# The sign factor of converted weight words: two VectorE comparisons, or two ScalarE signs and a GpSimd sum

## The chip, the cores and the metric

The kernel runs on one core of a Trainium2 chip. The core has five engines that run side by side, each through its own queue and strictly in the order written: TensorE (PE, matrix products, with its weight loads shown apart as PEld), VectorE (DVE), ScalarE (ACT), GpSimd (POOL) and SyncE (SP, which here only issues transfers). They wait for each other through semaphores. The metric is the device time of one execution in microseconds; lower is better.

## The reference

Three layers follow each other. Everything is float32, and the weights of the layers reach the kernel as float64 where the reference drew them so.

```python
scores = scale * np.matmul(q, k.transpose(0, 1, 3, 2))      # 4 x 8 heads, 576 x 576
thresh = np.max(scores, axis=-1, keepdims=True) - tau
scores = np.where(scores >= thresh, scores, -1e9)            # softmax over what is left, times v
...
expert_idx = np.argmax(x @ w_gate, axis=1)                   # one of 8 experts for each of 2304 tokens
h = np.maximum(xe @ w1[e], 0.0);  ye = h @ w2[e]             # 512 -> 1024 -> 512
out[mask] = gate_w[mask, None] * ye
...
h = x @ w_in                                                 # last layer, 512 -> 2048 -> 512
g = h - np.tanh(h)
return (g @ w_out).astype(np.float32)
```

`w_in` and `w_out` of the last layer are the subject here. They are float64 (the drawn float32 array is multiplied by a float64 scalar), so each weight comes in as two 32-bit words.

## The kernel before, in words

The program has three stages. Attention fills the time to about 345 us. A routing step (to about 370 us) sorts the tokens by expert. Then a loop over steps `g` runs the experts (`g` below `GE` = 72, from 370 to about 650 us) and the last layer (to the end). In one expert step PE computes `h` (L1040, 12 matmuls) for hidden block `g` and then `y` (L1095, 12 matmuls) for hidden block `g-2`. All products are made from a high and a low part of each factor, so every tile is split: ACT rounds to the high part, DVE or POOL subtracts to get the low part.

- `relu(g)`: ACT writes the high part `hh` from the PSUM tile `h` (L1075), DVE the low part `hl` (L1076: one operand in PSUM, one in SBUF). Only then is the PSUM tile free. `h` has two banks, so `h` of step `g+2` waits for L1076 of step `g`.
- `wload` (SP, L1002) and `wsplit`: weights of an expert are loaded four or five steps ahead and split two or three steps ahead (L1008 on ACT, L1010 on DVE for `w1` and on POOL for `w2`).
- `gather_exp` (POOL, L1057), `trans` (PE, L1017), `evac` (ACT L1027, DVE L1031) bring the next expert's tokens in.
- `conv`: the float64 words of the last layer's weights are turned into float32 in 32 chunks of 128 x 512 weights, and stored in DRAM (`wscr`) for the last layer. All 32 run between 370 and 627 us, in the expert stage, at steps written in the table `TB["conv"]`, with `TB["cv"]` = 0, 3, 4, 5: `load` at the chunk's step, `bits` three steps later, `sign` one after that, `store` one more.

In a chunk, `lo` and `hi` are the two words of each weight (every second element of the tile `cv`), `hf` is `hi` read as a float32, and `m` is half of the tile `cm`. `bits` builds the magnitude's bits in `lo` (L1155 writes a part into `m`, L1157 joins it with `lo`) and then starts the sign factor in `m`: L1159 writes 1 where `hf` is at most -T. `sign` takes the absolute value of the joined word on ACT (L1163), completes the factor on DVE (L1164: 1 where `hf` is at least T, less what L1159 wrote, so the factor is 1, -1 or 0), and multiplies both on POOL (L1166). `store` is an SP transfer (L1169) that waits for POOL; SP's weight loads for the next step stand behind it.

There is no scheduler: instructions stand on each engine's queue in the order in which the Python code emits them. Within a step this is `relu(g)`, then the list for the step (token evacuation, weight loads and splits, then the chunk's functions), then `y` of `g-2`. So on ACT what `sign` emits stands in front of the next step's L1075, and on DVE what `bits` emits stands in front of the next step's L1076.

Of the kernel before, what the change touches and what calls it, by code (L numbers as in the profile page):

```python
# [11 lines left out]
F32 = mybir.dt.float32  # L12
# [5 lines left out]
AF = mybir.ActivationFunctionType  # L18
ALU = mybir.AluOpType
# [447 lines left out]
class Moe:  # L467
# [110 lines left out]

    def hilo(self, T, x):
        V = self.nc.vector  # L580
        ab = T([128, 2, NTL], I32)
        V.tensor_scalar(out=ab[:, 0], in0=x, scalar1=7, scalar2=None, op0=ALU.logical_shift_right)
        V.tensor_scalar(out=ab[:, 1], in0=x, scalar1=127, scalar2=None, op0=ALU.bitwise_and)
        return ab[:, 0], ab[:, 1]

    def route(self, K, T, psum):

# [24 lines left out]
        cnt = self.cnt = inc[:, :, NTL]  # L612
        key, cmp, rank = T([128, E]), T([128, E, E]), T([128, E])
        sel, em = K([128, E, E]), T([128, E, E])
        self.sel = sel
        rm, rv = T([128, 2, E, E]), K([128, 2, E])
        self.eid = cp.tile([128, E], I32, name="eid")
# [295 lines left out]
def quads():  # L913

    r = sorted((x for x in np.roots(COEF[::-1]) if x.imag > 0), key=lambda x: x.real)
    return [float(v) for x in r for v in (-x.real, x.imag ** 2)] + [COEF[4]]


class Mlp(Moe):
    def run(self, ctx):  # L920
        nc, tc = self.nc, self.tc
        sp = self.sp = ctx.enter_context(tc.tile_pool(name="m", bufs=1))
        pp = self.pp = ctx.enter_context(tc.tile_pool(name="mp", bufs=1, space=PSUM))
        self.kn = quads()
        self.ab = self.cp.tile([128, 2], F32, name="kna")
        for i in range(2):
            nc.gpsimd.memset(self.ab[:, i:i + 1], self.kn[2 * i])
        self.sched, self.cm = {}, None
        self.hs, self.ys, self.W, self.xs, self.xr, self.evs, self.regs = {}, {}, {}, {}, {}, {}, {}
        self.keep = sp.tile([128, 3072], F32, tag="lxa", name="keep")  # L930
        self.free = sp.tile([128, max(6 * NMAX, 8 * NW)], F32, tag="lxb", name="free")
        K = Carve(self.keep)
        self.route(K, Carve(self.free), self.psum)
        self.hbuf = sp.tile([128, max(6 * NMAX, 8 * NW)], F32R, tag="lxb", name="hbuf")
        for fn in self.early():
            fn()
        for m in range(-(-PASS[0][2] // 128)):
            self.gather_exp(0, m, min(128, PASS[0][2] - 128 * m))
        self.early2()
        n = iter(range(12))  # L940
        self.overflow(lambda: sp.tile([128, 1024], F32R, **(dict(tag="xa", bufs=8) if next(n) < 8 else dict(tag="we", bufs=4)), name="wo"), self.psum)
        self.plan(K)
        g0 = int(min(self.sched)) - 1
        ny = g0 - LY
        for g in range(g0, GE + GL + 1):
            if g >= 0:
                if g < GE:
                    self.relu(g, g // 8, self.h_exp(g // 8, g % 8))
                elif g < GE + GL:
                    self.act(g, self.h_last(*divmod(g - GE, 16)))  # L950
                if GE < g <= GE + GL:
                    self.act2(g - 1)
            for fn, a in self.sched.get(g, []):
                fn(*a)
            if g - GE - GL + 16 in SKIP:
                ny -= 1
            elif LY <= g < GE + GL:
                self.y_mm(ny)
            ny += 1
            for fn, a in self.sched.get(g + 0.5, []):  # L960
                fn(*a)
        for g in range(ny - 1, GE + GL - MLAST):
            self.y_last(g)
        for m in range(MB):
            for g in range(GE + GL - MLAST, GE + GL):
                self.y_last(g, [m])
# [170 lines left out]

    def conv(self, i, h):
        nc = self.nc
        T = 3.4332275390625e-05  # L1140
        st = {}

        def load():
            t = self.sp.tile([128, 1024], F32R, tag="cv", name="cv", bufs=3).bitcast(U32)
            nc.sync.dma_start(out=t.rearrange("p (a b) -> p a b", a=2) if i < 8 else t, in_=self.src64[i][h])
            r = t.rearrange("p (n t) -> p n t", t=2)
            st["lo"], st["hi"] = r[:, :, 0], r[:, :, 1]
            st["hf"] = st["hi"].bitcast(F32)
            if self.cm is None:
                self.cm = self.sp.tile([128, 1024], F32R, tag="cm", name="cm")  # L1150
            st["m"] = self.cm.bitcast(F32)[:, 512 * h:512 * h + 512]

        def bits():
            m = st["m"].bitcast(U32)
            nc.vector.tensor_scalar(out=m, in0=st["hi"], scalar1=3, scalar2=0x40000000,  # L1155
                                    op0=ALU.logical_shift_left, op1=ALU.bitwise_xor)
            nc.vector.scalar_tensor_tensor(out=st["lo"], in0=st["lo"], scalar=29, in1=m,  # L1157
                                           op0=ALU.logical_shift_right, op1=ALU.bitwise_or)
            nc.vector.tensor_scalar(out=st["m"], in0=st["hf"], scalar1=-T, scalar2=None, op0=ALU.is_le)  # L1159

        def sign():
            c = st["lo"].bitcast(F32)
            nc.scalar.activation(out=c, in_=c, func=AF.Abs)  # L1163
            nc.vector.scalar_tensor_tensor(out=st["m"], in0=st["hf"], scalar=T, in1=st["m"],  # L1164
                                           op0=ALU.is_ge, op1=ALU.subtract)
            nc.gpsimd.tensor_tensor(out=st["m"], in0=st["lo"].bitcast(F32), in1=st["m"], op=ALU.mult)  # L1166

        def store():
            nc.sync.dma_start(out=self.wscr[i, :, 512 * h:512 * h + 512], in_=st["m"])  # L1169

        return [load, bits, sign, store]


# [185 lines left out]
```

## Time and profile before

| | |
|---|---|
| median of 3 runs | 1077.41 us (1076.29 to 1078.05) |
| the profiled execution | 1076.63 us |
| its span, first to last instruction | 1074.5 us |
| mean granted TensorE clock | 0.944 |
| busy over the span | PE 957.3, PEld 876.6, DVE 895.3, ACT 671.5, POOL 730.7 us |

The span is what the profile's times count from; 2.1 us of the execution lie around it. A busy share is an average over the whole program; the chunks' 32 instances of each instruction lie in the 270 us from 370 to 640, so that stretch is to be read apart. Two instructions on one engine may overlap by about 0.1 us at their borders, since the next one starts while the one before drains. A duration in the timeline begins when the engine starts an instruction, so time for which the instruction is held up inside, with no semaphore to wait for, is part of it.

### The profile page before, as it was taken

To read this page: it belongs to the slowest core of one execution; us is meant where nothing else is said; L and a number is where in the kernel's file an instruction comes from. 1 tells how busy PE (TensorE), PEld (TensorE's weight loads), DVE (VectorE), ACT (ScalarE), POOL (GpSimd) and SP (SyncE) were. 2 spreads that over 40 slices of the span, in tenths; PEclk is the share of its full clock that TensorE was granted. 3 is DMA by queue.
4 is the path that set the end of the run, shared out by engine and by line. 5 is a ranking of instruction groups with operands and counts; after the bars stand their busy time and mean duration, and the time that the engine had idled before them with its cause. 6 is when DMAs were issued, how large, how long until landed. Compare 5 with 4: busy or idle time off the path is not lost.

```text
span 1074.5 us, 20770 instructions
## 1 busy us (share of the span) xinstructions
PE 957.3 (89%) x7342; PEld 876.6 (82%) x7342; DVE 895.3 (83%) x1635; ACT 671.5 (62%) x1262; POOL 730.7 (68%) x645
## 2 busy tenths in 40 slices
PE   4688897887787488999999988999999999999997
PEld 3576786776677387989999988888999999998986
DVE  5899888888884698977798876998989889888894
ACT  5797887986974154444455557666665666656662
POOL 3897887886874364455656567787867768677763
PEclk9698888898988599999999999999999999999999
DMA  6798999998989485877787976220101101000000
GB/s 160 145 213 165 211 205 152 225 202 163 175 155 169 149 292 199 278 227 247 258 290 252 295 247 177 76 76 20 40 8 38 30 20 40 8 31 1 20 11 30
DMA packets 247368, 153.16 MB, mean 143 GB/s; under 512 B 179642, under 2 KB 222028, under 8 KB 247261
## 3 DMA queue, kind: packets, MB, share of 16 engines
q1 hardware_dynamic: 243501, 141.02, 53.2%
q0 software_dynamic: 3312, 10.49, 2.8%
q8 instruction: 59, 0.97, 0.4%
q14 instruction: 48, 0.39, 0.1%
q10 hardware_dynamic: 448, 0.30, 0.1%
HBM read 85.08 MB, written 23.60 MB: 101 GB/s over the span
## 4 chain that ended last, share of the span: by engine, by line
PE 50%; DVE 9%; issue 3%; DMA 2%; ACT 1%; POOL 0%; another core or an unknown queue 0%; POOLq 0%; DVEq 0%; SPq 0%; ACTq 0%
PE h L1040 25%; PE y L1123 15%; PE y L1095 9%; DVE w L1236 2%; DVE w L1237 2%; PE t L1017 1%; DVE w L1234 1%; DMA xr<-rows,idx 1%; DVE cv L1157 1%; DVE tm L1235 1%; DVE w L1238 1%; DMA raw<-in_moe_w_dram 1%; DVE w L1010 1%; DMA raw<-wscr 0%; DVE cm L1159 0%
## 5 line engine op out<-in xcount | busy, mean ns | idle before, releaser
L265 POOL TENSOR_TENSOR e<-em,e 128x1024 f16<-128x1024 f32 (+1 forms) x98 | 158.1, 1613 | 55.0 <-ACT e L261 23.5
L1233 POOL TENSOR_SCALAR tm<-u 128x384 uint8<-128x384 f32 x88 | 129.7, 1474 | 51.4 <-ACT u L1229 50.8
L1040 PE MATMUL h<-xa,w 128*128 128x256 f32 (+6 forms) x864 | 140.5, 313 | 7.6 <-DVE hbuf L1076 6.8
L1095 PE MATMUL y<-hbuf,w 128*128 128x256 f32 (+6 forms) x864 | 139.5, 310 | 0.6 <-ACT yo L1098 0.6
L1040 PEld LDWEIGHTS h<-xa,w 128*128 128x128 f32 x864 | 130.5, 194 | 9.9 <-DVE hbuf L1076 8.1
L240 ACT ACTIVATE e<-sps,n 128x576 f32<-128x576 f32 x144 | 110.6, 768 | 34.8 <-DVE n L234 33.7
L1010 POOL TENSOR_TENSOR w<-raw,w 128x1024 fp32r<-128x1024 f32 x36 | 91.8, 2551 | 56.0 <-ACT w L1008 28.8
L1095 PEld LDWEIGHTS y<-hbuf,w 128*128 128x128 f32 x864 | 127.5, 191 | 1.3 <-ACT yo L1098 0.8
L1236 DVE SCALAR_TENSOR_TENSOR w<-y,w 128x384 f32<-128x384 f32 x96 | 123.3, 1284 | 0.0
L1229 ACT ACTIVATE u<-h 128x384 f32<-128x384 f32 x96 | 47.1, 491 | 117.3 <-PE h L1040 116.4
L253 DVE SCALAR_TENSOR_TENSOR em<-sps,n,e 128x576 f32<-128x576 f32 x144 | 116.6, 810 | 4.0 <-ACT e L240 2.4
L234 DVE TENSOR_REDUCE n<-sps 128x1 f32<-128x576 f32 x144 | 107.1, 744 | 12.3 <-PE sps L226 11.8
L1250 POOL TENSOR_TENSOR gl<-w,gh 128x384 fp32r<-128x384 f32 x83 | 85.7, 1032 | 38.0 <-ACT gh L1249 38.0
L1040 PE MATMUL h<-xk,w 128*128 128x384 f32 x576 | 109.6, 338 | 0.7 <-DVE w L1010 0.5
L297 PE MATMUL ops<-vh,et 128*128 128x64 f16 (+1 forms) x2240 | 97.4, 201 | 13.0 <-DVE x L303 12.1
L1040 PEld LDWEIGHTS h<-xk,w 128*128 128x128 f32 x576 | 102.1, 188 | 5.6 <-DVE w L1010 1.3
L297 PEld LDWEIGHTS <-et 128*128 128x128 f16 (+1 forms) x2240 | 83.6, 107 | 25.3 <-issue 21.1
L261 ACT CAST e<-em 128x576 f16<-128x576 f32 x144 | 99.9, 695 | 1.2 <-DVE em L253 1.2
L1075 ACT ACTIVATE hbuf<-h 128x256 fp32r<-128x256 f32 (+6 forms) x72 | 31.2, 433 | 108.3 <-PE h L1040 108.2
L226 PE MATMUL sps<-ka,qa 128*128 128x288 f32 x320 | 87.7, 367 | 9.4 <-DVE em L253 5.7
L1008 ACT CAST w<-raw 128x1024 fp32r<-128x1024 f32 x72 | 75.6, 1051 | 21.4 <-DVE free L597 11.6
L1123 PE MATMUL y<-w,gh 128*128 128x512 f32 x258 | 81.1, 395 | 3.2 <-POOL w L1010 1.5
(228 smaller groups left out, 2296.8 us busy)
## 6 DMA issues: line engine op xcount, KB each, us to landing
raw<-in_moe_w_dram SPq DMA_DIRECT2D x64, 512.0 KB, 5.2
cv<-in_moe_w_in_dram SPq DMA_DIRECT2D x16, 512.0 KB, 5.0
cv<-in_moe_w_out_dram SPq DMA_DIRECT2D x16, 512.0 KB, 5.4
wscr<-cm SPq DMA_DIRECT2D x32, 256.0 KB, 3.2
raw<-wscr SPq DMA_DIRECT2D x16, 512.0 KB, 3.8
xw<-yT SPq DMA_DIRECT2D x24, 192.0 KB, 2.7
vv<-in_v_dram SPq DMA_DIRECT2D x8, 512.0 KB, 5.1
raw<-in_q_dram SPq DMA_DIRECT2D x6, 576.0 KB, 7.7
```

The source lines that it names most:

```text
L234: nc.vector.tensor_reduce(out=n[:, 0:1], in_=ps[:, :, 0:288], axis=AX.XY, op=ALU.max, negate=True)
L240: nc.scalar.activation(out=e, in_=ps[:, :, 0:288], func=AF.Exp, bias=n[:, 0:1])
L253: nc.vector.scalar_tensor_tensor(out=self.em[u, g][:, i].rearrange("p (a b) -> p a b", a=2), in0=ps[:, :, 0:288], scalar=n[:, 1:2], in1=e, ...
L261: self.nc.scalar.copy(self.e16[u, g][:, i, 0:S], self.em[u, g][:, i])
L265: eng.tensor_tensor(out=e16[:, r, S + 64:], in0=em[:, r, 0:512], in1=e16[:, r, 0:512], op=ALU.subtract)
L297: nc.tensor.matmul(o[q], lhsT=et[:, base + c, q], rhs=vh[:, a, j, c if c < 5 else c - 5, :], start=(n == 0), stop=(n == len(terms) - 1))
L1010: (self.nc.gpsimd if pool else self.nc.vector).tensor_tensor(out=l, in0=raw, in1=h.bitcast(F32), op=ALU.subtract)
L1040: self.nc.tensor.matmul(out, lhsT=a, rhs=b, start=(i == 0), stop=(i == len(parts) - 1))
L1095: nc.tensor.matmul(self.ys[d], lhsT=a[:, f % 2, s], rhs=b, start=(f == 0 and i == 0), stop=(f == 7 and i == 2))
L1123: nc.tensor.matmul(self.ys[m], lhsT=a[:, s], rhs=b[:, f % 2], start=(f == 0 and i == 0), stop=(f == 15 and i == 2))
L1233: nc.gpsimd.tensor_scalar(out=mk, in0=u, scalar1=RCUT * RCUT, scalar2=None, op0=ALU.is_gt)
L1236: V.scalar_tensor_tensor(out=w, in0=y, scalar=b, in1=w, op0=ALU.add, op1=ALU.mult)
```

## The change

Both DVE comparisons go. A small tile `knt` (`tt2`) gets two constants per partition, -T' and T', T' being the float32 just below T. In `sign`, ACT takes the sign of `hf` - T' into `m`, then the sign of `hf` + T' in place into `hf`, then the absolute value with the factor 0.5. POOL adds both signs (2, 0 or -2) and then multiplies as before. `bits` keeps L1155 and L1157.

```diff
@@ Mlp.run
+        T = float(np.nextafter(np.float32(3.4332275390625e-05), np.float32(0)))
+        self.tt2 = self.cp.tile([128, 2], F32, name="knt")
+        for i in range(2):
+            nc.gpsimd.memset(self.tt2[:, i:i + 1], T if i else -T)
@@ conv
-        T = 3.4332275390625e-05
@@ conv, bits
-            nc.vector.tensor_scalar(out=st["m"], in0=st["hf"], scalar1=-T, scalar2=None, op0=ALU.is_le)
@@ conv, sign
-            nc.scalar.activation(out=c, in_=c, func=AF.Abs)
-            nc.vector.scalar_tensor_tensor(out=st["m"], in0=st["hf"], scalar=T, in1=st["m"],
-                                           op0=ALU.is_ge, op1=ALU.subtract)
+            nc.scalar.activation(out=st["m"], in_=st["hf"], func=AF.Sign, bias=self.tt2[:, 0:1])
+            nc.scalar.activation(out=st["hf"], in_=st["hf"], func=AF.Sign, bias=self.tt2[:, 1:2])
+            nc.scalar.activation(out=c, in_=c, func=AF.Abs, scale=0.5)
+            nc.gpsimd.tensor_tensor(out=st["m"], in0=st["m"], in1=st["hf"], op=ALU.add)
             nc.gpsimd.tensor_tensor(out=st["m"], in0=st["lo"].bitcast(F32), in1=st["m"], op=ALU.mult)
```

The order of DVE before, at the chunk whose `bits` lie at 457.9 us in the profile (`hbuf<-h` is L1076, `w<-raw,w` the low part of an expert's weights, `keep` and `tok` small tiles of the routing):

```order
L1155 TENSOR_SCALAR cm<-cv 128x512
L1157 SCALAR_TENSOR_TENSOR cv<-cv,cm 128x512
L1159 TENSOR_SCALAR cm<-cv 128x512
L1076 SCALAR_TENSOR_TENSOR hbuf<-h,hbuf 128x416
L1010 TENSOR_TENSOR w_7274<-raw,w_7273 128x1024
L756 TENSOR_SCALAR keep<-h 128x18
L570 TENSOR_TENSOR tok_7383<-h,keep 128x18
L1164 SCALAR_TENSOR_TENSOR cm<-cv,cm 128x512
L1155 TENSOR_SCALAR cm<-cv 128x512
```

The same place on DVE now (line numbers are 3 or 4 higher: L1158 was L1155, L1160 was L1157, L1080 was L1076, L1014 was L1010):

```order
L1158 TENSOR_SCALAR cm<-cv 128x512
L1160 SCALAR_TENSOR_TENSOR cv<-cv,cm 128x512
L1080 SCALAR_TENSOR_TENSOR hbuf<-h,hbuf 128x416
L1014 TENSOR_TENSOR w_7286<-raw,w_7285 128x1024
L756 TENSOR_SCALAR keep<-h 128x18
L570 TENSOR_TENSOR tok_7396<-h,keep 128x18
L1158 TENSOR_SCALAR cm<-cv 128x512
```

The low part of the hidden tile now stands directly behind the second `bits` instruction, and nothing of `sign` is left on DVE.

ACT before, at the same place (L1163 is the absolute value, L1075 the high part of the hidden tile, L1008 an expert's weights):

```order
L1075 ACTIVATE hbuf<-h 128x416
L1008 CAST w_7273<-raw 128x1024
L1163 ACTIVATE cv<-cv 128x512
L1075 ACTIVATE hbuf<-h 128x416
L1027 CAST xa<-t 128x2x128 x2
```

ACT now (L1165 and L1166 are the two signs, L1167 the absolute value, L1079 was L1075):

```order
L1079 ACTIVATE hbuf<-h 128x416
L1012 CAST w_7285<-raw 128x1024
L1165 ACTIVATE cm<-cv,knt 128x512
L1166 ACTIVATE cv<-cv,knt 128x512
L1167 ACTIVATE cv<-cv 128x512
L1079 ACTIVATE hbuf<-h 128x416
L1031 CAST xa<-t 128x2x128 x2
```

Three instructions instead of one stand in front of the next step's hidden tile. On POOL each of the 32 multiplications gets the sum directly in front of it.

## Rows read from the trace of the kernel before

**Rows 1.** The profile page, the chain that ended last, by engine

```profile
PE 50%; DVE 9%; issue 3%; DMA 2%; ACT 1%; POOL 0%; another core or an unknown queue 0%; POOLq 0%; DVEq 0%; SPq 0%; ACTq 0%
```

**Rows 2.** Busy time by stretch: PE, PEld, DVE, ACT, POOL; granted clock; DMA share; GB/s

```profile
370.00:640.00 270.00, 255.53 (x1757) 250.67 (x1758) 223.01 (x320) 131.01 (x244) 152.36 (x89) 0.98 0.79 260
460.00:470.00 10.00, 7.47 (x39) 7.00 (x39) 9.60 (x14) 3.27 (x7) 5.13 (x5) 0.83 0.86 269
```

**Rows 3.** Waits of PE, 375 to 640 us: total, times, longest

```profile
PE h L1040 <- DVE hbuf L1076: 6.8, 4, 2.5
```

**Rows 4.** Groups, 375 to 640 us: count, busy us, mean ns, idle before

```profile
L1166 POOL TENSOR_TENSOR cm<-cv,cm 128x512 f32<-128x512 f32 x32 | 44.2, 1382 | 55.8 <-issue 16.6 <-ACT hbuf L1075 14.8 <-DVE cm L1164 9.9
...
L1159 DVE TENSOR_SCALAR cm<-cv 128x512 f32<-128x512 f32 x32 | 28.8, 900 | 1.1
L1164 DVE SCALAR_TENSOR_TENSOR cm<-cv,cm 128x512 f32<-128x512 f32 x32 | 28.4, 891 | 0.0
...
L1163 ACT ACTIVATE cv<-cv 128x512 f32<-128x512 f32 x32 | 22.0, 687 | 21.8 <-DVE cv L1157 12.4 <-issue 5.2 <-POOL cm L1166 3.4
```

**Rows 5.** Timeline at 459 us: start, duration, engine, instruction, idle before

```profile
459.06 1.83 PE L1095 MATMUL y<-hbuf,w 128*128 128x288 f32 x12
...
460.10 2.77 DVE L1159 TENSOR_SCALAR cm<-cv 128x512 f32<-128x512 f32 x1
...
460.21 2.36 POOL L1010 TENSOR_TENSOR w<-raw,w 128x1024 fp32r<-128x1024 f32 x1
...
462.79 0.58 DVE L1076 SCALAR_TENSOR_TENSOR hbuf<-h,hbuf 128x416 fp32r<-128x416 f32 x1
...
463.42 4.09 PE L1040 MATMUL h<-xa,w 128*128 128x416 f32 x12 [2.53 <-DVE hbuf L1076]
...
469.40 2.44 PE L1040 MATMUL h<-xa,w 128*128 128x416 f32 x12
```

**Rows 6.** Timeline, POOL beside L1076, at 416 us

```profile
416.19 2.60 POOL L1010 TENSOR_TENSOR w<-raw,w 128x1024 fp32r<-128x1024 f32 x1 [4.64 <-ACT w L1008]
...
418.34 0.42 DVE L1076 SCALAR_TENSOR_TENSOR hbuf<-h,hbuf 128x256 fp32r<-128x256 f32 x1 [1.81 <-ACT hbuf L1075]
```

**Rows 7.** ScalarE with and without a per-partition bias: ns min/median/max

```profile
L1230 ACT ACTIVATE y<-u,kna x96: 615/617/622, 653.1 to 1053.7; 128x384 f32<-128x384 f32 x96
```

**Rows 8.** The same columns, a cast of the same size without bias

```profile
L1249 ACT CAST gh<-w x83: 497/500/518, 658.4 to 1010.1; 128x384 fp32r<-128x384 f32 x83
```

**Rows 9.** Timeline at 619 us, the last two chunks

```profile
619.25 0.69 ACT L1163 ACTIVATE cv<-cv 128x512 f32<-128x512 f32 x1 [3.11 <-DVE cv L1157]
...
621.07 0.45 DVE L1076 SCALAR_TENSOR_TENSOR hbuf<-h,hbuf 128x288 fp32r<-128x288 f32 x1
621.35 0.41 ACT L1075 ACTIVATE hbuf<-h 128x288 fp32r<-128x288 f32 x1
...
621.57 1.85 PE L1040 MATMUL h<-xa,w 128*128 128x288 f32 x12 [2.17 <-DVE hbuf L1076]
```

**Rows 10.** Timeline at 408 us, the first change of expert

```profile
408.09 0.43 DVE L1159 TENSOR_SCALAR cm<-cv 128x512 f32<-128x512 f32 x1
...
409.62 1.09 PE L1017 MATMUL t<-ident,xr 128*128 128x128 f32 x4 [4.46 <-issue]
```

**Rows 11.** Timeline at 390 us, the second chunk

```profile
389.69 2.50 DVE L1159 TENSOR_SCALAR cm<-cv 128x512 f32<-128x512 f32 x1
...
390.28 0.37 ACT L1075 ACTIVATE hbuf<-h 128x256 fp32r<-128x256 f32 x1
...
392.57 1.70 PE L1040 MATMUL h<-xa,w 128*128 128x256 f32 x12 [1.47 <-DVE hbuf L1076]
```

**Rows 12.** Waits of SP's queue, 375 to 640 us: total, times, longest

```profile
SPq L1169 <- POOL cm L1166: 108.2, 29, 9.5
```

**Rows 13.** The two memsets of the tile kna: ns min/median/max

```profile
L927 POOL MEMSET kna<- x2: 99/99/99, 335.5 to 335.6; 128x1 f32 x2
```

**Rows 14.** Timeline, POOL's first work after the routing's start

```profile
357.97 1.00 POOL L654 TENSOR_TENSOR free<-free,tok 128x468 f16<-128x468 f32 x1 [22.29 <-DVE free L597]
```

## Prediction

> **What bounds the kernel now.** I began with the chain of waits on the page: half of the span is PE work, a tenth DVE work [rows 1]. The reader is to see there that PE sets the pace, but not everywhere. The edit touches only the 32 chunks between 370 and 640 us, so next comes the busy time of that stretch [rows 2]: in 270 us PE is busy for 255.5, DVE for 223, POOL for 152 and ACT for 131. PE is the bound of the stretch, and the most that any edit of the other engines can return directly is its idle time, 14.5 us. The third view is what PE waited for. The largest entry is L1040 waiting for DVE's L1076, 6.8 us in four waits, the longest 2.5 [rows 3]. L1076 is the low part of the hidden tile, and it stands on DVE directly behind what `bits` emits. So the fourth view is the timeline at those waits. At 460.10 DVE starts L1159, which takes 2.77 us instead of its own 0.43 [rows 5, 10]: POOL started L1010 0.11 us later and ran until 462.57, and L1159 ended 0.30 us after that. L1076 follows at 462.79 and PE at 463.42, after 2.53 us of idleness. The groups tell that this is common: L1159 takes 0.43 us undisturbed and 0.90 on the mean, L1164 0.89 [rows 4, 10].
>
> L1076 itself is not held by POOL: one that ran beside L1010 took 0.42 us and ended before L1010 did [rows 6]. The Trainium skill, SBUF — State Buffer, section "Who interferes with whom", says that a DVE instruction with two SBUF inputs, or in a two-port mode, and a GpSimd instruction that reads SBUF shut each other out for a whole instruction, while a DVE instruction with one SBUF input goes free. The trace agrees for L1159 and for L1076 [rows 5, 6].
>
> **What is removed.** 32 L1159 and 32 L1164, 28.8 + 28.4 = 57.2 us of DVE [rows 4]. Of this 32 x 0.43 = 13.8 us is L1159's own work. Nearly all of it lies beside PE's matmuls and is worth nothing. What is worth something is DVE time directly ahead of an L1076 or L1031 that PE waits for. I go through those places.
>
> *At 463 us.* L1159 goes, and L1076 follows L1157, which ended when L1159 began, at 460.10. But on POOL the chunk before now has a sum ahead of its product, so L1155 and L1157 can be held by one POOL instruction more. I let L1157 end 0.4 us later, at 460.5; L1076 takes 0.58 and PE could go on at about 461.2. The `y` matmuls in front of it end at 459.06 + 1.83 = 460.89 [rows 5]. 0.3 us of the 2.53 is left: 2.2 us gained. Besides, the 12 matmuls after the wait took 4.09 us and the same 12 six us later 2.44 [rows 5], in a stretch whose mean granted clock is 0.83 [rows 2]; of the clock's two levels, 2.4 and 1.2 GHz, PE had dropped to the lower after its idle time. With 0.3 us of idleness I expect the higher: 1.65 us more. Together 3.9 us.
>
> *At 621 us.* Two L1159 go from in front of L1076, 0.86 us of the 2.17 that PE waited [rows 9, 10]. Against it stands ACT: both chunks' `sign` stand in front of L1075 at 621.35, and this L1075 moves to about 623.4 (below), L1076 behind it to 624.3, just as the next `h` wants its bank. I count 0.4 us gained.
>
> *At 409 us.* PE waits 4.46 us before the token transposes, since DVE comes late to L1031, the evacuation of the tile before. One L1159 (0.43) stands in that row of DVE work [rows 10]: 0.4 us gained.
>
> *At 392 us.* L1159 was held to 392.19 and PE waited 1.47 us [rows 11]. L1075, at 390.28 before, now has two signs in front of it, so it ends near 392.1 instead of 390.65, and L1076 can begin no earlier than it did. 0.3 us lost.
>
> **What is added on ACT.** The absolute value takes 0.69 us in a chunk [rows 4]. The trace has no sign. From below I take the absolute value's 0.69, since the tile and the strided reading are the same; from above 0.69 plus the price of a per-partition bias, 617 - 500 = 117 ns by two rows of one size [rows 7, 8], so 0.80. I take 0.80. As neighbours overlap by 0.1 us (L1163 from 619.25 to 619.94 is such a duration), each sign keeps the queue for 0.7, a chunk for 2.1 instead of 0.69: 1.4 us more, 45 us in 32 chunks. ACT goes from 131 to 176 of 270 us [rows 2]. What hides it is that L1075 mostly waits for PE anyway, and that what L1075 releases is wanted only when the other `h` bank and two rounds of `y` are through: three pieces of some 1.8 us [rows 5, 9], about 5 us. Cost taken: nothing, apart from the two places above. Without that cover it is 1.4 us for each chunk; the worst place is 619.25, where six instructions, 4.2 us, start late because the first of them waits for L1157, as L1163 does before [rows 9].
>
> **What is added on POOL.** The sum has the product's shape and one stride less. Bounds: 1.38 us, the product's mean, or, if held by DVE as much as the other, some 2 us. I take 1.38: 44 us in all, POOL from 152 to 196 of 270 [rows 2, 4]. POOL was idle before the 32 products for 55.8 us in sum, waiting for ACT's or DVE's last part of the chunk [rows 4]; L1164 was that last part in several chunks and is gone, so a product ends about 1.4 us later where POOL was the late one and up to L1164's own 0.9 earlier where L1164 was; a few tenths later on the mean. SP's stores wait for the product in 29 cases [rows 12], with the next weight loads behind them, and the gathers stand behind it on POOL. Those loads run steps ahead; cost taken: nothing, with 1 us at most where a change of expert has a gather close to its transposes.
>
> The Trainium skill, GPSIMD Engine Reference, opening section, speaks against moving plain elementwise work to that engine: the Vector engine is about twice as fast. Here the trace agrees, 1.38 us against L1164's 0.89, though both means hold some time of being held [rows 4]. By that page the edit is a loss of engine time; by the rows it is one only where POOL or ACT is what PE waits for.
>
> Two memsets of 0.1 us [rows 13] stand in front of L654, where POOL idles 22 us for the routing [rows 14]; uncovered 0.2 us.
>
> **Sum.** 3.9 + 0.4 + 0.4 - 0.3 = 4.4 us less than the profiled execution's 1076.63: 1072.2. The median of the runs is 0.8 above that execution, so the forecast is 1073.0. All later stages are reached earlier and pass the gain on, since PE runs almost without gaps in the last layer.
>
> **Rivals.**
>
> *No change.* The sum holds POOL's side of the port 1.38 us longer in each chunk, and the DVE instructions that remain (L1155, L1157, L1010) are held instead of L1159. At 460 us L1157 would then end near 462.3 instead of 460.5, PE would go on at 463.0, and the slow clock stays: the 3.9 us shrink to 0.4, the sum to 0.9, the time to 1076.5. For it speaks that each removed hold was followed by more port users; against it that L1076 now stands one port user earlier.
>
> *Larger gain.* DVE loses 57 us of 223 and is early everywhere: all four waits (6.8), the one at 409 (4.5) and the slow clock (1.65) go. 1077.4 - 13 = 1064.5. Against it: at 392 ACT takes over, and at 409 the holds by POOL's L1010 are not touched.
>
> *Slower, by ACT.* Where L1163 already waits for L1157, the two signs start late and L1075 stands behind them. ACT's idle time in front of L1163 is 21.8 us in sum [rows 4]. If in 9 of the 32 chunks L1075 comes so late that PE waits the added 1.4 us, that is 12.6 us against the gain of 4.4: 1077.4 + 8.2 = 1085.6. It decides from five such places on (7.0 us, 2.6 slower). For it: ACT's queue is in order and the worst place has 4.2 us in a row. Against: 5 us of slack between L1075 and its use, and no wait of PE for L1075 in the trace.
>
> **How the numbers follow.** Forecast (2.2 to 8 us less) 0.51, no change 0.24, larger gain 0.10, slower 0.15. A measurement tells 0.2%, 2.15 us, from no change. So faster 0.61, same 0.24, slower 0.15. The likeliest case alone spans 1069 to 1075. The range, with no change, a part of the larger gain (half of its 13 us beyond 1073 would be 1066) and the near side of the slower case, is 1066 to 1079.5.
>
> **What would show it.** Right: in the new profile PE's wait at the place of 463 us is under 0.6 us and the matmuls behind it take 2.4 us; the total of L1040's waits for L1076 falls from 6.8 to about 3; DVE's busy time between 370 and 640 is some 45 us lower, ACT's 45 higher, POOL's 44 higher; a sign takes 0.8 us and the sum 1.4. Wrong: new waits of L1040 or L1095 in which the tile's ACT instruction had come late, new waits of L1017 for gathers, or longer L1155 and L1157 that eat up what L1159 gave back.

## The result and the profile after

The changed kernel takes 1084.43 us (median of 8 runs, 1083.04 to 1091.75). The kernel before, run 8 times beside it, takes 1078.15 us (1076.29 to 1080.91). The ratio is 1.0068, with a 95% interval of 1.0045 to 1.0090: the change makes the kernel 6 to 7 us slower. The forecast was 1073.0 us, faster, and the time lies above its range.

The profiled execution of the changed kernel took 1086.87 us (span 1085.2), 2.4 us above its median. Its first hidden tile of the expert stage comes 2.7 us later than before, ahead of the first chunk. Three other kernels that share the changed front part start within 0.8 us of before, so I don't count this 2.7 as the change's.

In the code after, the new lines are L1165 and L1166 (the signs), L1167 (the absolute value), L1168 (the sum) and L1169 (the product, L1166 before). The other lines that matter moved by 3 or 4: L1158 was L1155, L1160 was L1157, L1172 was L1169 (store), L1014 was L1010, L1012 was L1008, L1006 was L1002, L1021 was L1017, L1035 was L1031, L1044 was L1040, L1079 and L1080 were L1075 and L1076, L1099 was L1095.

The page's chain by engine, which answers to [rows 1]:

```profile
PE 46%; DVE 9%; issue 3%; ACT 3%; DMA 2%; POOL 2%; another core or an unknown queue 0%; SPq 0%; POOLq 0%; DVEq 0%; ACTq 0%
```

Four points of the chain left PE; ACT and POOL have two more each. The two stretches of [rows 2], after (busy time of PE, PEld, DVE, ACT and POOL, then granted clock, DMA share, GB/s). The second is moved by the 7.1 us that step 24 is late here (table below), so that it holds the same steps:

```profile
370.00:640.00 270.00, 250.60 (x1678) 243.95 (x1677) 178.02 (x250) 168.13 (x296) 196.59 (x119) 0.96 0.75 247
467.10:477.10 10.00, 7.62 (x49) 7.17 (x47) 9.82 (x10) 5.48 (x10) 9.72 (x6) 1.00 0.86 266
```

DVE has 45.0 us less, ACT 37.1 more, POOL 44.2 more. PE is busy for 4.9 us less in the same 270 us, at a lower clock. The second stretch is the place where I had looked for the gain. The clock there is full now (1.00, before 0.83), but PE is busy for 7.62 us, hardly more than the 7.47 before: one wait has gone and another has come, as the timeline below shows. What PE waited for, 375 to 650 us (total, times, longest), beside [rows 3]:

```profile
PE t L1021 <- issue: 9.2, 3, 5.5
PE h L1044 <- ACT w L1012: 3.1, 2, 2.5
PE t L1021 <- DMA xr<-rows,idx: 2.8, 1, 2.8
PE h L1044 <- DVE w L1014: 1.5, 2, 0.8
PE h L1044 <- DVE hbuf L1080: 0.8, 1, 0.8
```

The waits for the low part of the hidden tile fell from 6.8 to 0.8 us, more than I forecast. In their place stand waits in front of the token transposes (9.2 in three places; before, 4.46 in one [rows 10]) and for expert weights (3.1 and 1.5).

Where the time is lost is seen by following one instruction, L1075 before and L1079 after, step by step. The table gives its start in each kernel less its start in the kernel before, us; the two right columns are experiments told below.

```
step  before at   after   sum on DVE   no sum
 0     373.49      +2.7      +0.8       -0.0
 9     400.13      +2.8      +0.6       -1.6
10     409.76      +5.9      +1.9       -3.6
24     458.85      +7.1      +2.0       -5.9
25     467.61      +2.8      -2.3      -10.2
26     471.94      +7.2      +0.1       -8.5
60     611.49      +7.0      -1.4      -10.6
62     621.35     +13.0      +1.0       -8.8
71     649.11     +10.9      -1.1      -11.1
```

The change loses some 3 us at step 10, gains 4.3 at step 25 and gives 4.4 back at step 26, and loses some 4 at the end. Such a start holds ACT's own lateness too, so a single row can be off by a microsecond or two; the levels last (step 11 is 5.5 us late, step 27 is 7.0). Here is step 25, the place of [rows 5], in the timeline after:

```profile
466.20 1.83 PE L1099 MATMUL y<-hbuf,w 128*128 128x288 f32 x12
...
467.20 0.58 DVE L1080 SCALAR_TENSOR_TENSOR hbuf<-h,hbuf 128x416 fp32r<-128x416 f32 x1
...
467.87 2.51 PE L1044 MATMUL h<-xa,w 128*128 128x416 f32 x12
```

No wait stands at the matmuls of L1044, where 2.53 us stood, and they take 2.51 instead of 4.09. Nine microseconds on, behind the hidden tile of step 26, the gain is lost (columns as in [rows 5]):

```profile
467.70 3.94 DVE L1014 TENSOR_TENSOR w<-raw,w 128x1024 fp32r<-128x1024 f32 x1
...
468.14 2.41 POOL L1014 TENSOR_TENSOR w<-raw,w 128x1024 fp32r<-128x1024 f32 x1
...
471.87 2.24 DVE L1158 TENSOR_SCALAR cm<-cv 128x512 uint32<-128x512 uint32 x1
...
472.49 1.33 POOL L1168 TENSOR_TENSOR cm<-cm,cv 128x512 f32<-128x512 f32 x1
...
473.90 1.38 POOL L1169 TENSOR_TENSOR cm<-cv,cm 128x512 f32<-128x512 f32 x1
474.15 1.68 DVE L1160 SCALAR_TENSOR_TENSOR cv<-cv,cm 128x512 uint32<-128x512 uint32 x1
...
475.75 0.58 DVE L1080 SCALAR_TENSOR_TENSOR hbuf<-h,hbuf 128x416 fp32r<-128x416 f32 x1
...
476.25 0.74 DVE L1035 TENSOR_TENSOR xa<-t,xa 128x256 fp32r<-128x256 f32 x2
...
477.09 0.63 PE L1021 MATMUL t<-ident,xr 128*128 128x128 f32 x4 [2.38 <-issue]
...
477.47 4.17 PE L1099 MATMUL y<-hbuf,w 128*128 128x416 f32 x12
```

Read the DVE rows against the POOL row beside each. L1014 takes 3.94 us beside POOL's L1014 (undisturbed, 1.22). L1158 takes 2.24 and ends 0.3 us after the sum; undisturbed it takes 0.42. L1160 takes 1.68 beside the product (0.69). The three holds cost DVE 5.5 us. Not all of that is the sum's. In the kernel without the sum (an experiment below, where L1168 is the product) the same instructions read:

```profile
454.45 2.53 DVE L1014 TENSOR_TENSOR w<-raw,w 128x1024 fp32r<-128x1024 f32 x1 [0.34 <-ACT w L1012]
...
457.22 2.24 DVE L1158 TENSOR_SCALAR cm<-cv 128x512 uint32<-128x512 uint32 x1
...
457.84 1.32 POOL L1168 TENSOR_TENSOR cm<-cv,cm 128x512 f32<-128x512 f32 x1
...
459.49 0.69 DVE L1160 SCALAR_TENSOR_TENSOR cv<-cv,cm 128x512 uint32<-128x512 uint32 x1
```

There the product holds L1158 just as long, but no second instruction of the chunk stands behind it, and L1160 takes its own 0.69. The holds cost 3.1 us there, 2.4 less. With the sum, then, L1035, the evacuation that frees the bank for the next transposes, comes that much later. PE idles 2.38 us, and its next 12 matmuls run at the lower clock (granted 0.58 from 477.5 to 481.6 us): 4.17 us for what took 2.51 before and 2.87 in the kernel without the sum. Step 10 reads the same way:

```profile
403.11 3.43 DVE L1014 TENSOR_TENSOR w<-raw,w 128x1024 fp32r<-128x1024 f32 x1 [0.51 <-ACT w L1012]
...
405.52 2.19 POOL L1169 TENSOR_TENSOR cm<-cv,cm 128x512 f32<-128x512 f32 x1
...
406.46 1.42 DVE L570 TENSOR_TENSOR u<-O,keep 128x144 f32<-128x144 f16 x1
...
407.86 0.91 POOL L1061 DMA_INDIRECT xr<-rows,idx  x1
...
408.34 2.85 DVE L570 TENSOR_TENSOR keep<-keep 128x18 int32<-128x18 f32 x1
...
408.79 2.36 POOL L1014 TENSOR_TENSOR w<-raw,w 128x1024 fp32r<-128x1024 f32 x1
...
413.64 1.08 PE L1021 MATMUL t<-ident,xr 128*128 128x128 f32 x4 [5.53 <-issue]
```

A small routing instruction, L570 at 408.34, is held for 2.85 us, and PE waits 5.53 us at a place where it had waited 4.46 [rows 10]. That hold was there before as well:

```profile
403.41 0.30 DVE L570 TENSOR_TENSOR u<-O,keep 128x144 f32<-128x144 f16 x1
...
404.19 2.52 DVE L570 TENSOR_TENSOR keep<-keep 128x18 int32<-128x18 f32 x1
```

What is new stands in front of it: L1014 takes 3.43 us (2.26 as L1010 before), and the other L570 1.42 beside the product (0.30 before). Near the end something else shows, in front of the last weights of the experts:

```profile
617.77 1.22 SPq L1006 DMA_DIRECT2D raw<-in_moe_w_dram  x2
...
624.69 1.04 ACT L1012 CAST w<-raw 128x1024 fp32r<-128x1024 f32 x1 [5.76 <-DMA raw<-in_moe_w_dram]
...
625.79 0.53 PE L1044 MATMUL h<-xa,w 128*128 128x288 f32 x2 [2.51 <-ACT w L1012]
```

SP issues this load 2.15 us after the hidden tile of step 59 (615.62); before, it was 0.8 us after (607.99 after 607.19). The loads arrive after the cast is due. In SP's queue they stand behind a store that waits for the product: the product in front ends at 612.94, 2.7 us ahead of that hidden tile, where before it ended at 602.94, 4.3 us ahead. Last, the groups that answer to [rows 4], after, 375 to 650 us (count, busy us, mean ns, idle before), and below them two of the kernel before, 375 to 640 us:

```profile
L1169 POOL TENSOR_TENSOR cm<-cv,cm 128x512 f32<-128x512 f32 x32 | 51.2, 1600 | 2.5
L1168 POOL TENSOR_TENSOR cm<-cm,cv 128x512 f32<-128x512 f32 x32 | 46.2, 1445 | 23.8 <-ACT cv L1166 23.7
L1160 DVE SCALAR_TENSOR_TENSOR cv<-cv,cm 128x512 uint32<-128x512 uint32 x32 | 38.9, 1215 | 1.1
L1158 DVE TENSOR_SCALAR cm<-cv 128x512 uint32<-128x512 uint32 x32 | 27.1, 848 | 4.7 <-DMA wscr<-cm 1.8 <-POOL cm L1168 1.5 <-POOL cm L1169 1.4
L1166 ACT ACTIVATE cv<-cv,knt 128x512 f32<-128x512 f32 x32 | 24.7, 772 | 2.8
L1165 ACT ACTIVATE cm<-cv,knt 128x512 f32<-128x512 f32 x32 | 24.6, 768 | 23.3 <-DVE cv L1160 23.3
```

```profile
L1157 DVE SCALAR_TENSOR_TENSOR cv<-cv,cm 128x512 uint32<-128x512 uint32 x32 | 41.7, 1303 | 1.1
...
L1155 DVE TENSOR_SCALAR cm<-cv 128x512 uint32<-128x512 uint32 x32 | 21.6, 674 | 0.3 <-DMA wscr<-cm 0.3
```

A sign takes 0.77 us and the sum 1.45; the product slowed from 1.38 to 1.60. The two instructions of the chunk that stayed on DVE were not freed: L1158 stands at 848 ns, and at 674 as L1155 before; L1160 at 1215, and at 1303 as L1157.

### The profile page after: what moved, and what is told of

It reads as the page before. It is cut to its first block, busy times and chain, and to the rows that moved or that the text cites. A ratio compares the mean times of both kernels' runs of the same rounds, so it can differ in the third digit from the quotient of the medians.

```text
span 1085.2 us, 20787 instructions
## 1 busy us (share of the span) xinstructions
PE 958.9 (88%) x7342; PEld 877.4 (81%) x7342; DVE 857.5 (79%) x1571; ACT 713.5 (66%) x1326; POOL 779.8 (72%) x679
## 4 chain that ended last, share of the span: by engine, by line
PE 46%; DVE 9%; issue 3%; ACT 3%; DMA 2%; POOL 2%; another core or an unknown queue 0%; SPq 0%; POOLq 0%; DVEq 0%; ACTq 0%
PE h L1044 23%; PE y L1127 15%; PE y L1099 8%; DVE w L1239 2%; DVE w L1240 2%; DMA raw<-in_moe_w_dram 1%; DVE w L1237 1%; PE t L1021 1%; DVE w L1014 1%; DVE tm L1238 1%; ACT cm L1165 1%; POOL w L1014 1%; DVE cv L1160 1%; ACT w L1012 1%; POOL cm L1169 1%
## 5 line engine op out<-in xcount | busy, mean ns | idle before, releaser
L1044 PE MATMUL h<-xa,w 128*128 128x256 f32 (+6 forms) x864 | 141.5, 314 | 6.4 <-ACT w L1012 3.1
L1099 PE MATMUL y<-hbuf,w 128*128 128x256 f32 (+6 forms) x864 | 142.7, 315 | 0.4 <-ACT yo L1102 0.4
L1044 PEld LDWEIGHTS h<-xa,w 128*128 128x128 f32 x864 | 131.0, 195 | 8.8 <-ACT w L1012 3.6
L1099 PEld LDWEIGHTS y<-hbuf,w 128*128 128x128 f32 x864 | 130.2, 194 | 1.6 <-ACT yo L1102 1.0
L1239 DVE SCALAR_TENSOR_TENSOR w<-y,w 128x384 f32<-128x384 f32 x96 | 123.6, 1287 | 0.0
L1014 POOL TENSOR_TENSOR w<-raw,w 128x1024 fp32r<-128x1024 f32 x36 | 92.1, 2558 | 41.8 <-ACT w L1012 41.6
L1044 PE MATMUL h<-xk,w 128*128 128x384 f32 x576 | 109.4, 338 | 2.0 <-DVE w L1014 1.8
L1044 PEld LDWEIGHTS h<-xk,w 128*128 128x128 f32 x576 | 102.2, 188 | 6.7 <-DVE w L1014 2.4
L1012 ACT CAST w<-raw 128x1024 fp32r<-128x1024 f32 x72 | 75.7, 1053 | 23.9 <-DVE free L597 11.7
L1080 DVE SCALAR_TENSOR_TENSOR hbuf<-h,hbuf 128x256 fp32r<-128x256 f32 (+6 forms) x72 | 34.5, 480 | 71.8 <-ACT hbuf L1079 71.5
L1240 DVE SCALAR_TENSOR_TENSOR w<-y,w 128x384 f32<-128x384 f32 x96 | 77.5, 808 | 10.7 <-DVE w L1239 0.9
```

Of the source, the lines that this page charges most:

```text
L1014: (self.nc.gpsimd if pool else self.nc.vector).tensor_tensor(out=l, in0=raw, in1=h.bitcast(F32), op=ALU.subtract)
L1044: self.nc.tensor.matmul(out, lhsT=a, rhs=b, start=(i == 0), stop=(i == len(parts) - 1))
L1099: nc.tensor.matmul(self.ys[d], lhsT=a[:, f % 2, s], rhs=b, start=(f == 0 and i == 0), stop=(f == 7 and i == 2))
L1239: V.scalar_tensor_tensor(out=w, in0=y, scalar=b, in1=w, op0=ALU.add, op1=ALU.mult)
```

## The experiments

Three theories. *A*: ACT's longer queue costs the time (the slower rival of the prediction). *H*: the GpSimd sum holds out DVE's instructions, and they reach PE late. *S* or *Q*: the sum costs by its own time in POOL's queue, behind which stand product, store, SP's loads and the gathers. *P* in the expectations is H and S taken together. Ratios are to the kernel before, run beside each, with a 95% interval.

**Sum of the signs on VectorE.**

```diff
-            nc.gpsimd.tensor_tensor(out=st["m"], in0=st["m"], in1=st["hf"], op=ALU.add)
+            nc.vector.tensor_tensor(out=st["m"], in0=st["m"], in1=st["hf"], op=ALU.add)
```

> The changed kernel with the sum of the two signs on VectorE instead of GpSimd; ScalarE does the same three instructions. Theory P (the GpSimd sum costs the time: it makes the product, and with it SP's store and the weight loads behind, later, and it holds VectorE's two-input instructions out): 1074 to 1079 us, and none of the waits of TensorE at 625 and 477 us. Theory A (ScalarE's two signs in front of the casts and the hidden tile cost it): 1082 to 1087 us, as the changed kernel.

1077.71 us, ratio 1.0002 (0.9983 to 1.0021): as before. ACT does the same as in the changed kernel, so A can't be the loss; P's range holds. The sum on POOL costs some 7 us more than the sum on DVE, where it takes 984 ns.

**One sign, without bias and without a sum.** Words below the smallest normal float32 are no longer set to zero.

```diff
-            nc.scalar.activation(out=st["m"], in_=st["hf"], func=AF.Sign, bias=self.tt2[:, 0:1])
-            nc.scalar.activation(out=st["hf"], in_=st["hf"], func=AF.Sign, bias=self.tt2[:, 1:2])
-            nc.scalar.activation(out=c, in_=c, func=AF.Abs, scale=0.5)
-            nc.gpsimd.tensor_tensor(out=st["m"], in0=st["m"], in1=st["hf"], op=ALU.add)
+            nc.scalar.activation(out=st["m"], in_=st["hf"], func=AF.Sign)
+            nc.scalar.activation(out=c, in_=c, func=AF.Abs)
```

> The changed kernel with one sign on ScalarE and no sum: the factor is 1 or -1, and what is below float32's normal range is no longer set to zero (this part of the computation is left out). ScalarE has 0.7 us more per chunk than before, GpSimd nothing more, VectorE 57 us less. Theory P: 1071 to 1076 us, faster than before. Theory A: half of the loss, 1080 to 1083 us.

1062.63 us, ratio 0.9864 (0.9839 to 0.9889). Taking the comparisons from DVE is worth 15 us when no sum comes with it: near the rival "larger gain" (1064.5), not the forecast. P's range (1071 to 1076) was missed on the low side. Its group of signs gives the price of the bias:

```profile
L1165 ACT ACTIVATE cm<-cv 128x512 f32<-128x512 f32 x32 | 21.7, 678 | 10.2 <-DVE cv L1160 10.2
```

**The kernel before with a GpSimd sum ahead of each product.** The sum's result isn't used.

```diff
+            nc.gpsimd.tensor_tensor(out=st["hf"], in0=st["m"], in1=st["hf"], op=ALU.add)
             nc.gpsimd.tensor_tensor(out=st["m"], in0=st["lo"].bitcast(F32), in1=st["m"], op=ALU.mult)
```

> The kernel before with one more GpSimd instruction per chunk, a sum of the same shape and strides in front of the product; VectorE and ScalarE as before. Theory P: 1084 to 1090 us, at least the loss of the change, since VectorE keeps its two comparisons. Theory A: 1076 to 1080 us.

1100.98 us, ratio 1.0226 (1.0200 to 1.0252): 23.6 us slower, more than P's range (1084 to 1090). PE's waits, 375 to 640 us:

```profile
PE t L1017 <- issue: 13.4, 5, 5.5
PE t L1017 <- DVE xa L1031: 4.1, 1, 4.1
PE h L1040 <- DVE hbuf L1076: 3.5, 4, 1.1
PE h L1040 <- DVE w L1010: 3.3, 3, 1.5
```

The same places as in the changed kernel, the transposes above all, and larger. The sum does it with no sign on ACT.

**The kernel before with the absolute value taken three times**, 1.4 us more of ACT in each chunk.

```diff
             nc.scalar.activation(out=c, in_=c, func=AF.Abs)
+            nc.scalar.activation(out=c, in_=c, func=AF.Abs)
+            nc.scalar.activation(out=c, in_=c, func=AF.Abs)
```

> The kernel before with ScalarE's absolute value done three times in place, so that ScalarE has 1.3 us more per chunk in front of the product and of the next hidden tile; GpSimd and VectorE as before. Theory P: 1076 to 1081 us. Theory A: 1084 to 1090 us.

1080.4 us, ratio 1.0022 (1.0006 to 1.0039): 45 us of ACT work cost about 2.4 us. A is refuted as the main cause; the prediction's "nothing" was nearly right for ACT.

**The store a step later**, in the changed kernel and, as its control, in the kernel before.

```diff
-"cv": (0, 3, 4, 5)
+"cv": (0, 3, 4, 6)
```

> The changed kernel with every chunk's store one step later (last entry of the table of offsets 6 instead of 5), so that SP has a step more before it waits for GpSimd's product, and weight loads are no longer behind a product that is late. Theory S (of GpSimd's sum, the part that counts is that the product comes late to SP's store): 1077 to 1081 us, without the wait of TensorE at 625 us. Theory H (what counts is that the sum holds out VectorE's instructions with two inputs, so that the token evacuation is late): 1083 to 1087 us, as the changed kernel.

> The control to the one before: the kernel before with every chunk's store one step later. Theory S: nothing to repair, or a little, 1074 to 1079 us. Theory H: 1076 to 1079 us.

1091.83 us (1.0135, 1.0108 to 1.0161) and 1079.93 us (1.0022, 1.0008 to 1.0036). The first lies above both ranges, and this answers nothing on S. With the store later, the half of `cm` that it reads comes free too late, and DVE waits for it (17.4 us in the control, 33.8 in the changed kernel). In the changed kernel with the late store, 375 to 640 us:

```profile
DVE cm L1158 <- DMA wscr<-cm: 33.8, 12, 4.9
```

A version with a second pair of halves, which would mend that, wasn't run.

**The kernel before with two GpSimd memsets ahead of each product**, 627 + 582 = 1209 ns, with nothing read.

```diff
+            nc.gpsimd.memset(st["hf"], 0.0)
+            nc.gpsimd.memset(st["hf"], 0.0)
             nc.gpsimd.tensor_tensor(out=st["m"], in0=st["lo"].bitcast(F32), in1=st["m"], op=ALU.mult)
```

> The kernel before with two GpSimd memsets of 128x512 (every second word) per chunk in front of the product, where the run before had a sum: they occupy GpSimd's queue but read nothing. The sum in that place cost 23.6 us. Theory H: with some 1.4 us of memsets per chunk at most a third of it, up to 1085 us, since VectorE's instructions with two inputs go on beside a memset. Theory S: two thirds or more, 1093 us and up, if the memsets take as long as the sum; the time taken is read from the profile.

1081.13 us, ratio 1.0026 (1.0012 to 1.0040): 3.7 us, where the sum of 1397 ns in the same place cost 23.6. On the kernel before, POOL's queue time is the small part and the reading the large one, as H has it.

**The changed kernel without the sum.** The product takes one sign alone; the second sign stays on ACT, unused.

```diff
-            nc.gpsimd.tensor_tensor(out=st["m"], in0=st["m"], in1=st["hf"], op=ALU.add)
```

> The changed kernel without the GpSimd sum; the product takes one sign alone, so the second sign and the sum are left out of the values. This prices the whole sum inside the change. If the sum is what the change pays for (my theory), the time falls to about that of the kernel with one sign, 1062.6 us, plus 1 to 3 us for the second sign on ACT: 1063 to 1067. If ACT's three instructions were the cost, it stays above 1078.

1067.00 us, ratio 0.9906 (0.9891 to 0.9921). The whole sum costs 17.4 us in the changed kernel. The right column of the table above is this kernel: it gains at step 10 and at step 25, and keeps nearly all of both. The two places, from its timeline:

```profile
404.26 0.60 PE L1021 MATMUL t<-ident,xr 128*128 128x128 f32 x4
...
461.50 0.60 PE L1021 MATMUL t<-ident,xr 128*128 128x128 f32 x4
...
461.85 2.87 PE L1099 MATMUL y<-hbuf,w 128*128 128x416 f32 x12
```

Neither transpose has a wait, and the matmuls run at the higher clock (granted 1.00).

**The changed kernel with two memsets in place of the sum** (580 + 567 = 1147 ns; the sum is left out).

```diff
-            nc.gpsimd.tensor_tensor(out=st["m"], in0=st["m"], in1=st["hf"], op=ALU.add)
+            nc.gpsimd.memset(st["hf"], 0.0)
+            nc.gpsimd.memset(st["hf"], 0.0)
```

> The changed kernel with two GpSimd memsets of the strided half `hf` (about 1.2 us together, they read no tile) in place of the sum of about 1.4 us. The sum is left out of the values. If the sum costs by holding VectorE's instructions out while GpSimd reads (H), the memsets cost little, as on the kernel before (3.7 us there): 1066 to 1071. If it costs by GpSimd's own queue time, which makes product, store and the weight loads behind it late (Q), nearly the whole price stays: 1080 to 1084.

1075.83 us, ratio 0.9977 (0.9960 to 0.9994): between H (1066 to 1071) and Q (1080 to 1084), so neither alone. The memsets cost 8.8 us of the 17.4, the rest, 8.6, is what a reading sum adds; part of that is its 0.3 us of greater length. If queue time counts in proportion, 8.8 x 1445 / 1147 = 11.1 us are POOL's queue and 6.3 the holding: an estimate.

That split goes by what is added, not by the way it reaches PE. DVE's busy time from the first hidden tile to the last (L1075 or L1079 of step 0 to step 71) says more, since within each group of three rows what is added lies on POOL alone and DVE has the same work (246 instructions in each of the last three rows, 308 to 310 recorded in the first three):

| kernel | length, us | DVE busy, us | POOL busy, us |
|---|---|---|---|
| before | 275.62 | 224.99 | 157.29 |
| before, two memsets | 279.51 | 224.64 | 196.75 |
| before, sum | 295.53 | 255.88 | 208.11 |
| changed, no sum | 264.53 | 158.64 | 154.51 |
| changed, two memsets | 274.90 | 172.26 | 191.09 |
| changed (sum) | 283.76 | 185.86 | 207.72 |

On the kernel before, the memsets lengthen DVE's work by nothing, and they cost little. On the changed kernel they lengthen it by 13.6 us, half of the sum's 27.2, although they themselves read nothing: L1160 takes 1234 ns on the mean beside 991 without them. So a part of what is counted as queue here is again DVE held, by POOL's reading instructions (the product, L1014), which the memsets move to other times. Why this happens here and not on the kernel before isn't shown; one difference is that the sum and all behind it wait for ACT's second sign, 23.7 us in the 32 chunks of the changed kernel.

What the memset doesn't do is seen in one pair of rows of this kernel:

```profile
498.83 0.58 POOL L1168 MEMSET cv<- 128x512 f32 x1 [1.84 <-ACT cv L1166]
498.87 0.69 DVE L1160 SCALAR_TENSOR_TENSOR cv<-cv,cm 128x512 uint32<-128x512 uint32 x1
```

L1160, with two inputs, takes its own 0.69 us beside a memset, in all seven such places where no other GpSimd work overlaps it; beside the product at 474.15 it took 1.68. The Trainium skill, SBUF — State Buffer, section "Who interferes with whom", says so: a DVE instruction with two SBUF inputs is shut out only by a GpSimd instruction that reads SBUF. The trace agrees.

**The sign bit joined on VectorE**, one instruction in place of L1159, L1164 and the GpSimd product. Words below the smallest normal float32, zero too, are not set to zero.

```diff
-            nc.vector.tensor_scalar(out=st["m"], in0=st["hf"], scalar1=-T, scalar2=None, op0=ALU.is_le)
...
-            nc.vector.scalar_tensor_tensor(out=st["m"], in0=st["hf"], scalar=T, in1=st["m"],
-                                           op0=ALU.is_ge, op1=ALU.subtract)
-            nc.gpsimd.tensor_tensor(out=st["m"], in0=st["lo"].bitcast(F32), in1=st["m"], op=ALU.mult)
+            nc.vector.scalar_tensor_tensor(out=st["m"].bitcast(U32), in0=st["hi"], scalar=0x80000000, in1=st["lo"],
+                                           op0=ALU.bitwise_and, op1=ALU.bitwise_or)
```

> A chunk without a factor: VectorE takes the sign bit out of the high word and joins it to the absolute value in one instruction with two inputs (in the place of L1164), GpSimd does nothing for the chunk. What is below float32's normal range, zero among it, is not set to zero (left out). VectorE 29 us less than before, ScalarE as before, GpSimd 44 us less. Theory P: faster than the version with one sign (1062.6), as GpSimd's 44 us are free: 1055 to 1062 us. Theory A: ScalarE is as before, so only VectorE's gain, 1070 to 1077 us.

1057.86 us, ratio 0.9828 (0.9807 to 0.9848), the fastest. Its busy times from 370 to 640 us (columns as above):

```profile
370.00:640.00 270.00, 267.97 (x1887) 264.89 (x1887) 196.02 (x300) 141.52 (x263) 115.67 (x62) 0.99 0.82 273
```

DVE is busier than in the changed kernel (196 against 178), POOL far less (116 against 197), and PE has 2 us of idleness left. DVE's busy time alone doesn't decide; against the kernel before a comparison and the product went together, so the run doesn't part their shares.

**The same, with the small words set to zero.** ACT takes the absolute value of `hf` too, and DVE sets the word to zero by it; the whole computation is kept.

```diff
+            nc.scalar.activation(out=st["m"], in_=st["hf"], func=AF.Abs)
             nc.scalar.activation(out=c, in_=c, func=AF.Abs)
+            nc.vector.scalar_tensor_tensor(out=c, in0=st["m"], scalar=3.4332275390625e-05, in1=c,
+                                           op0=ALU.is_ge, op1=ALU.mult)
```

> The sign bit joined on VectorE as in the kernel at 1057.9 us, with the flush of small words kept: ACT takes a second absolute value (of `hf`), VectorE sets the word to zero where that is below the threshold and then joins the sign bit; the GpSimd product is gone. The whole computation is kept. VectorE gets some 22 us back against the kernel at 1057.9, ACT 22 us. If GpSimd's reading is what holds VectorE, and its own work is hidden, 1058 to 1064; if VectorE's own busy time is what counts, near the kernel before, 1072 to 1078, since its busy time is then about that of before.

1070.49 us, ratio 0.9938 (0.9919 to 0.9957): of the kernels that keep the whole computation, the only one that beats the kernel before, by 7 us. The time fell between my two guesses. DVE's work is not free either: this one instruction and its ACT partner cost 12.6 us against the kernel above.

## Why the prediction was wrong

**The step that failed** is "What is added on POOL", with its "Those loads run steps ahead; cost taken: nothing, with 1 us at most". The sum's length was right (1.38 taken, 1.45 measured). Its price is 17.4 us. I had looked for the sum's cost in POOL's own lateness and found it a few tenths per chunk. Apart from 0.4 us at 463 I did not price what the sum does to DVE. The same 246 DVE instructions take 27.2 us longer with it: beside the sum and the product L1158 and L1160 are held, and L1014 and L570 by POOL's reading instructions that now stand at other times. Through them the evacuations that PE's transposes wait for come late. And the sum takes 1.4 us from the gathers, stores and loads behind the product. The reading of POOL's idle time was too broad as well: of the 55.8 us in front of the products, [rows 4] puts 9.9 on L1164 and 16.6 on no wait at all.

**A second step was too small: "What is removed".** I summed 4.4 us over four places. The kernel without the sum gains 10.5 us (1077.46 less 1067.00), its two signs included. With both terms put right the sum gives 1073.0 - 6.1 + 17.4 = 1084.3, measured 1084.43; both terms come from that one kernel, so this has to close and proves nothing by itself.

*At 463 us* (3.9 forecast): right. Wait and slow clock went, step 25 gained 4.3, though the holds there were larger than the 0.4 taken (L1158 1.16 us, L1160 1.68): L1080 ended at 467.78, just ahead of the `y` matmuls' end at 468.03. That the gain would last was wrong, in the changed kernel: "All later stages are reached earlier and pass the gain on" looked at the last layer and left out the transposes nine microseconds on.

*At 409 us* (0.4 gained): wrong on both sides. Without the sum, PE's wait of 4.46 us goes altogether; with it, it grows to 5.53. I had credited only the one removed L1159 in the row and had read the holds by POOL's L1010 as fixed, though they come and go as GpSimd's work shifts by a microsecond or two: L570 is held where POOL's weight split starts 0.11 us (before) or 0.45 us (after) behind it, and takes its own 0.18 in the kernel without the sum, where the split starts 2.0 us behind it.

*At 392 us* (0.3 lost) and *at 621 us* (0.4 gained): too small to tell. The total of the hbuf waits, 0.8, bounds any loss there; at the end the weight load's lateness covers the place.

**What is added on ACT**: right. A sign takes 0.77 us (0.80 taken), and no wait of PE names the tile's ACT instruction L1079. The bias makes 0.09 us (768 against 678), where I took 0.117 from [rows 7, 8]. The Trainium skill, ScalarE: Activation LUTs, section "What ACT_TABLE_LOAD costs", gives about 93 ns for such an operand; the trace agrees.

**The rivals.** The slower one gave 1085.6, almost the time measured, by the wrong engine: its mechanism, ACT, costs some 2 us by the experiment with three absolute values. "No change" named a mechanism that does act, the sum's hold on L1155, L1157 and L1010, and priced it at one place only, 463 us, where it acts but PE has nothing to wait for; it should have been priced as a loss in all 32 chunks, with the transposes as what becomes late. "Larger gain" was what the removal is worth with no sum.

**What stays open**: how the 17.4 us divide between holding and queue (about 6 and 11 by an estimate from the memsets, though DVE's busy time says that a part of the 11 is holding too), and how much of the queue's part comes by stores and weight loads, and how much by gathers; the late store didn't test it. The memsets' cost comes in two parts: against the kernel without the sum, L1079 starts 4.4 us later at step 24, 5.2 at step 55 and 10.1 at step 70.

## What to carry to other kernels

Where VectorE and GpSimd work side by side on SBUF, price an instruction moved to GpSimd by the VectorE work that it can hold and by what stands behind it in both queues, not by whether GpSimd has idle time. A split that adds a step to combine its halves has to pay for that step: here the combination cost more (17.4 us) than the split saved (10.5). When a wait is removed, look at the next two or three places where the same engine is late, since the gain is only kept if they are not.

## What was not expected of the hardware

- A GpSimd instruction of 1.40 us that reads two tiles cost 23.6 us over the 32 chunks on the kernel before; two memsets of 1.21 us together cost 3.7.
- VectorE's single-input L1155, 0.42 us undisturbed, is held by a memset that started first (0.57, 0.60 and 0.78 us at the three places with nothing but memsets beside it), while the two-input L1157 right behind it stays at 0.69 (the kernel before with two memsets).
- Two memsets ahead of each product lengthened VectorE's own unchanged work by 13.6 us in the changed kernel, and by nothing in the kernel before.
- Between two GpSimd instructions that stand back to back (472.49 and 473.90), VectorE's waiting L1158 seems to have got through: it ended at 474.11, 0.2 us after the second had started.
- On strided 128x512 tiles the sum takes 984 ns on VectorE, held time included, and 1445 ns on GpSimd.
